# Batch 0's q and k as cast loads on the GpSimd queue, with one planner for the order: a change to a fused attention and channel-mix kernel

## The chip, the cores and the metric

The kernel runs on one core of one Trainium2 chip. The metric is the device time of one execution in microseconds (us). Shown are the median of three runs and one profiled execution, whose trace is what all times of instructions below come from.

A core has five instruction streams that matter here. TensorE (PE in the profile; its weight loads are PEld) multiplies matrices into PSUM. VectorE (DVE), ScalarE (ACT) and GpSimd (POOL) compute on tiles. SyncE (SP) only issues DMAs. POOL issues DMAs too, and it is the stream on which a DMA is issued that changes the type on its way (float32 in memory, bf16 in the tile). Each stream executes its instructions in the order in which they stand in the program.

## The reference, cut to what matters

```python
B, N, C = 4, 6208, 256
qn = q / (norm(q, axis=1) + 1e-6)          # norm over the 6208 rows, per column
kn = k / (norm(k, axis=1) + 1e-6)
a  = softmax(kn.T @ qn / tau)              # 256 x 256 for each batch
x  = v @ a                                 # 6208 x 256 for each batch
x_prev = shift x by one row (zero first)
xk = mu_k * x + (1 - mu_k) * x_prev        # xr with mu_r
out = sigmoid(xr @ w_r) * (relu(xk @ w_k) ** 2 @ w_v)
```

Each of q, k, v and the output is 4 x 6208 x 256 float32. The softmax of a batch needs all of that batch's q and k, and every row of that batch's output needs that softmax.

## The kernel before, in words

**Tiling.** Rows are handled in blocks of 512: 12 blocks per batch and 64 rows left over in each, the leftovers of the four batches together making one more block. That gives 49 blocks (`NBLK`). For a block `n`, `v_load` brings v by a cast DMA on POOL, `v_turn_pe` (first blocks) or `v_turn_dma` (later ones, a transposing DMA on SP) turns it, `x_stage` computes x = v a, `mix_stage` builds xk and xr on DVE, `up_stage` does the product with w_k, the relu on ACT and the square on DVE, `down_stage` the products with w_r and w_v, the tanh, the product and the store.

**The head.** Nothing of a block's chain can start before batch 0's softmax `A[0]`. So the kernel begins with a loop over `order0`, a list of loads of q and k of batch 0 in groups of 512 rows (28 loads; a group is 512 KB, the last k group comes in three pieces and the 64 leftover rows are small loads). Each is a float32 DMA on SP into one of ten buffers `f32s` (L280), a cast to bf16 on DVE (L291), a square on ACT or DVE (L297, L300), and products on PE: the covariance k.T q into `s_ps` (L313) and the sums of squares by a product with ones into `vr` (L306, L319), eight small products per load.

After the last q comes `inverse` and `spread` ("rq"): a power on POOL (L239, the square root of the summed squares), a few tiny steps on DVE, six small products on PE that spread q's factors over all partitions, and a copy to `rq`. After the last k, `softmax(0)`: the norms of k through POOL's L239 again, the scaling on DVE (L372), the exponential on ACT (L386), and `A[0]` on DVE (L393). Then x of block 0 (L427, copied out at L434 and L437), the mix (L467, L475, L484), and the first up product (L513).

**The other batches.** `cov_group(b, g)` loads q and k of batch `b`, group `g`, as cast DMAs on POOL (L622) into pairs made of the same buffers `f32s`, squares them on ACT (L634), adds the squares up on DVE and does products for covariance and norms (L650, L657). These are spread over the time of the earlier batch's blocks.

**What sets the order.** The program's order on every engine is written by a planner. Each step is given an engine, a duration, a key and the tiles that it reads and writes. `Plan.order` is a greedy list scheduler: whenever an engine is free in its model, it takes, of all steps whose inputs are ready, the one with the lowest key. A key is a priority, not an earliest time: a step with a late key is taken at once where the engine has nothing else that is ready. A DMA costs its engine an issue time, and its data arrive later by a bandwidth model; how many DMAs can be under way at a time is not part of the model. The steps are then put into the program in the order of their modelled starts.

In the head a fourth argument keeps steps back: the loads of v, of the weights and of batch 1 carry `after=gate_w`, which makes each of them depend on the fourth last cast of the head:

```python
gate_w = [s for s in cast_done if s.name == "cast0"][-4:-3]
gate_qk = gate_w
v_load(0, KC - 2, after=gate_w)
...
writes=[("qk", gi, x)], size=rows * n * C * 4, name="ld qk", after=list(gate_qk) + list(head))
```

Of the kernel before, what the change touches and what calls it, by code (L numbers as in the profile page):

```python
# [17 lines left out]
class Step:  # L18
    __slots__ = ("eng", "dur", "out", "key", "fn", "deps", "users", "left", "ready", "start", "seq", "size", "name")


class Plan:
# [3 lines left out]
    WAIT = {"PE": 0.3, "ACT": 0.12, "DVE": 0.12, "POOL": 0.15, "SP": 0.0}  # L26

    def __init__(self):
        self.steps = []
        self.writer = {}  # L30
        self.readers = {}

    def add(self, eng, dur, key, fn, reads=(), writes=(), size=0, name="", after=()):
        s = Step()
        s.eng, s.dur, s.key, s.fn, s.size, s.name = eng, dur, key, fn, size, name
        s.seq = len(self.steps)
        s.deps, s.users = set(after), []
        for r in reads:
            if r in self.writer:
                s.deps.add(self.writer[r])  # L40
            self.readers.setdefault(r, []).append(s)
        for w in writes:
            if w in self.writer:
                s.deps.add(self.writer[w])
            for r in self.readers.get(w, ()):
                s.deps.add(r)
            self.writer[w] = s
            self.readers[w] = []
        s.deps.discard(s)
        self.steps.append(s)  # L50
        return s

    RATE = 395e3
    MOVE = 1.3
    LAND = 0.8

    def order(self):
# [6 lines left out]
        free = {e: 0.0 for e in self.WAIT}  # L64
        waiting = {e: [] for e in self.WAIT}
        able = {e: [] for e in self.WAIT}
        bus = 0.0
# [4 lines left out]
        while len(done) < len(self.steps):  # L72
            best = None
            for e in free:
# [6 lines left out]
                if best is None or t < best[0]:  # L81
                    best = (t, e)
            t, e = best
            while waiting[e] and waiting[e][0][0] <= t:
# [4 lines left out]
            end = t + s.dur  # L89
            free[e] = end  # L90
            if s.size:
                bus = max(bus, end + self.MOVE) + s.size / self.RATE
                end = bus + self.LAND
            s.out = end
            done.append(s)
            for u in s.users:
                lag = 0.0 if s.size else (0.02 if u.eng == e else self.WAIT[e])
                u.ready = max(u.ready, end + lag)
# [7 lines left out]
def pe(n):  # L106
    return n / 2400 + 0.0025


def act(n, ptr=0):  # L110
    return 0.17 + n / 1200 + 0.09 * ptr


def dve(n, mode=1):
    return 0.16 + n / 960 / mode
# [3 lines left out]
def kernel(  # L119
# [13 lines left out]
    nc = tc.nc  # L133
# [12 lines left out]

    sb = ctx.enter_context(tc.tile_pool(name="sb", bufs=1))
# [10 lines left out]
    ones = sbuf("ones", [P])  # L158
# [9 lines left out]
    NF, NQ0, NK0 = 10, 8, 3  # L168
    f32s = ring("f32s", NF, [S, C], F32)
    q0 = ring("q0", NQ0, [S, C])  # L170
    k0 = ring("k0", NK0, [S, C])
    s0 = ring("s0", 3, [S, C])
# [13 lines left out]
    NV, NT = 4, 4  # L186
# [22 lines left out]
    T = 9.7  # L209
    KC = -2.0 * T - 8.0  # L210

    make_identity(nc, ident)
    nc.vector.memset(ones, 1.0)
    nc.vector.memset(half, 0.5)
    nc.vector.tensor_copy(ident_f, ident)

# [6 lines left out]
    LEAD = 7  # L223
# [10 lines left out]
    H0 = -100.0  # L234

    def inverse(i, key, srcn, sres, lo, hi, name):

        nres = ("nq" if lo == 0 else "nk", i)
        add("POOL", 0.8, key + .01, lambda: nc.gpsimd.tensor_tensor(nrm[i][:, lo:hi], srcn[:, lo:hi], half[:, lo:hi], op=OP.pow),  # L239
            reads=[(sres, i)], writes=[nres], name=name + " pow")  # L240
        add("DVE", dve(4), key + .02, lambda: nc.vector.tensor_scalar_add(nrm[i][:, lo:hi], nrm[i][:, lo:hi], 1e-6),
            reads=[nres], writes=[nres], name=name)
        rw = [("rrq", i)] if hi == 2 else [("rrk", i)] if lo == 2 else [("rrq", i), ("rrk", i)]
        add("DVE", dve(4), key + .03, lambda: nc.vector.reciprocal(rr[i][:, lo:hi], nrm[i][:, lo:hi]),
            reads=[nres], writes=rw, name=name)
        if inv_tau != 1.0 and hi == 4:
            add("DVE", dve(4), key + .03, lambda: nc.vector.tensor_scalar_mul(rr[i][:, 2:4], rr[i][:, 2:4], inv_tau),
                reads=[("rrk", i)], writes=[("rrk", i)], name=name)

    def spread(i, key, name):  # L250

        h, m, l = (rb[x][i] for x in range(3))
        w = [("rb", i)]
        add("DVE", dve(2), key + .04, lambda: nc.vector.tensor_copy(h, rr[i][:, 0:2]), reads=[("rrq", i)], writes=w, name=name)
        add("DVE", dve(2), key + .05, lambda: nc.vector.tensor_tensor(rd[i], rr[i][:, 0:2], h, op=OP.subtract),
            reads=[("rrq", i)] + w, writes=[("rd", i)], name=name)
        add("DVE", dve(2), key + .06, lambda: nc.vector.tensor_copy(m, rd[i]), reads=[("rd", i)], writes=w, name=name)
        add("DVE", dve(2), key + .07, lambda: nc.vector.tensor_tensor(l, rd[i], m, op=OP.subtract),
            reads=[("rd", i)] + w, writes=w, name=name)

        def go():
            for hh in range(2):
                for x, term in enumerate((h, m, l)):
                    nc.tensor.matmul(xp[:, hh * P:(hh + 1) * P], term[:, hh:hh + 1].to_broadcast([P, P]), ident,
                                     start=x == 0, stop=x == 2)
        add("PE", 6 * pe(P), key + .08, go, reads=w, writes=[("xp",)], name=name)
        add("DVE", dve(C), key + .09, lambda: nc.vector.tensor_copy(rq[i], xp[:, :C]), reads=[("xp",)], writes=[("rq", i)], name=name)

    fslot = 0
    slot0 = {}  # L270
    nsq = 0
    for i, (tn, g, j0, j1) in enumerate(order0):
        key = H0 + i
        t = q if tn == "q" else k
        rows = P if g < NB else L
        fs = fslot % NF
        fslot += 1
        f = f32s[fs]
        n = j1 - j0
        add("SP", 0.45, key, lambda f=f, t=t, g=g, j0=j0, j1=j1, rows=rows: nc.sync.dma_start(  # L280
            f[:rows, j0:j1], src(t, 0, g)[:, j0:j1, :]), writes=[("f", fs)], size=rows * n * C * 4, name="ld0")
        if tn == "q":
            ci = g % NQ0
            cast, cres = q0[ci], ("q0", ci)
        else:
            ci = g % NK0
            cast, cres = k0[ci], ("k0", ci, j0)
        wr = [cres]
        if tn == "k" and j0 == 0:
            wr = [("k0", ci, 0), ("k0", ci, 2), ("k0", ci, 3)] if g != NB - 1 else [("k0", ci, 0)]  # L290
        add("DVE", dve(n * C, 2), key, lambda f=f, cast=cast, j0=j0, j1=j1, rows=rows: nc.vector.tensor_copy(  # L291
            cast[:rows, j0:j1], f[:rows, j0:j1]), reads=[("f", fs)], writes=wr, name="cast0")
        si = nsq % 3
        nsq += 1
        s2 = s0[si]
        if tn == "k" and g < NB - 1 and g % 2 == 1:
            add("DVE", dve(n * C, 2), key + 0.5, lambda s2=s2, cast=cast, j0=j0, j1=j1, rows=rows: nc.vector.tensor_tensor(  # L297
                s2[:rows, j0:j1], cast[:rows, j0:j1], cast[:rows, j0:j1], op=OP.mult), reads=[cres], writes=[("s0", si)], name="sq0")
        else:
            add("ACT", act(n * C), key, lambda s2=s2, f=f, j0=j0, j1=j1, rows=rows: nc.scalar.activation(  # L300
                s2[:rows, j0:j1], f[:rows, j0:j1], AF.Square), reads=[("f", fs)], writes=[("s0", si)], name="sq0")
        if tn == "q":
            for j in range(j0, j1):
                def go(s2=s2, j=j, rows=rows, st=(i == 0 and j == 0)):
                    for ih in range(2):
                        nc.tensor.matmul(vr[1][:, ih:ih + 1], s2[:rows, j, ih * P:(ih + 1) * P], ones[:rows, 0:1],  # L306
                                         start=st and ih == 0, stop=False, skip_group_check=True)
                add("PE", 0.13, key + 0.3, go, reads=[("s0", si)], writes=[("vr", 1)], name="nq0")
        else:
            for j in range(j0, j1):  # L310
                def go(ci=ci, g=g, j=j, rows=rows):
                    for ih in range(2):
                        nc.tensor.matmul(s_ps[:, ih, :], k0[ci][:rows, j, ih * P:(ih + 1) * P], q0[g % NQ0][:rows, j],  # L313
                                         start=g == 0 and j == 0 and ih == 0, stop=False, skip_group_check=True)
                add("PE", 2 * pe(C), key + 0.1, go, reads=[cres, ("q0", g % NQ0)], writes=[("s_ps",)], name="cov0")

                def go(s2=s2, j=j, rows=rows, st=(g == 0 and j == 0)):
                    for ih in range(2):
                        nc.tensor.matmul(vr[0][:, ih:ih + 1], s2[:rows, j, ih * P:(ih + 1) * P], ones[:rows, 0:1],  # L319
                                         start=st and ih == 0, stop=False, skip_group_check=True)  # L320
# [452 lines left out]
```

## Time and profile before

| what | value |
|---|---|
| median of 3 runs (lowest to highest) | 528.32 us (528.12 to 529.24) |
| span of the profiled execution, first to last instruction | 526.0 us |
| what lies outside that span: median less span | 2.3 us |
| PE busy in the span | 491.1 us (93%) |
| DVE, ACT, POOL busy | 417.8 (79%), 398.5 (76%), 88.7 (17%) |
| DMA queue of POOL (q0), of SP (q1): time of their packets | 43.1%, 36.5% of 16 engines' span |
| PE busy from 60 to 510 us, from 0 to 30, from 30 to 60 | 441.3 of 450, 14.9 of 30, 23.7 of 30 |
| first up product (L513) begins | 51.22 us |

The page of a profile gives busy times, the chain of waits that ended last, and the costliest groups of instructions; the trace behind it answers for any stretch of time what every engine did and what it waited for. POOL's row counts its DMA issues (`DMA_DIRECT2D`) as work. "us to landing" is the time from the issue of a DMA to the moment at which its data are reported to be there.

### The profile page before, as it was taken

Reading aid. Unit: us, or ns where it says so; the run is one execution under the profiler, and the core shown is the slowest. Engines: PE = TensorE matmul, PEld = TensorE weight load, DVE = VectorE, ACT = ScalarE, POOL = GpSimd, SP = SyncE. Lnnn points to the kernel's source line nnn. Section 1 sums busy time; section 2 is a strip of 40 time slices with the busy share of each in tenths; the row PEclk is TensorE's granted clock in tenths of the full one; section 3 lists DMA queues with packets and bytes.
Section 4 is the critical chain, followed back from the end, with each engine's and each line's share of the span. In section 5 each row is a group of like instructions: output and inputs, shape, how many; then the busy total and the mean of one; then the engine's idle time right before and its main releaser. Section 6 shows DMA issues by size and latency. Waiting matters only on the chain.

```text
span 526.0 us, 9943 instructions
## 1 busy us (share of the span) xinstructions
PE 491.1 (93%) x3707; PEld 342.7 (65%) x3761; DVE 417.8 (79%) x970; ACT 398.5 (76%) x573; POOL 88.7 (17%) x148
## 2 busy tenths in 40 slices
PE   1785999999899999999999999999999999999996
PEld 1563777756567767666667776666666666666674
DVE  4565997788879877798888778798888887878873
ACT  6543999788789978877898868877776787777763
POOL 0054433331123233211111210010010100000000
PEclk9998999999999999999999999999999999999999
DMA  8999999999999999998758854556465563413123
GB/s 333 402 312 206 205 187 203 197 203 206 212 191 133 205 188 161 210 215 128 127 106 145 147 90 92 126 102 145 97 99 143 105 143 81 121 40 102 41 81 100
DMA packets 113944, 83.23 MB, mean 158 GB/s; under 512 B 49572, under 2 KB 101352, under 8 KB 113896
## 3 DMA queue, kind: packets, MB, share of 16 engines
q0 software_dynamic: 38160, 33.01, 43.1%
q1 hardware_dynamic: 75736, 49.59, 36.5%
q8 instruction: 29, 0.48, 0.4%
q14 instruction: 19, 0.16, 0.1%
HBM read 78.71 MB, written 25.43 MB: 198 GB/s over the span
## 4 chain that ended last, share of the span: by engine, by line
PE 77%; DVE 7%; DMA 7%; issue 4%; ACT 3%; POOL 2%; SPq 0%; ACTq 0%; POOLq 0%
PE vr L551 28%; PE kT L513 28%; PE vr L546 7%; PE xp L427 6%; PE s_ps L650 6%; DMA f32s<-in_q_dram 3%; ACT kr L516 2%; DMA f32s<-in_k_dram 2%; DMA vT<-v_bf 2%; DVE kk L518 2%; DVE dm L475 1%; DVE res L557 1%; DVE dl L467 1%; DVE xk L484 1%; POOL v_bf L335 1%
## 5 line engine op out<-in xcount | busy, mean ns | idle before, releaser
L551 PE MATMUL vr<-w_v,kk 128*128 128x256 bf16 x1552 | 251.3, 273 | 1.0
L516 ACT ACTIVATE kr<-kT 128x1024 bf16<-128x1024 f32 (+1 forms) x200 | 198.6, 1001 | 53.2 <-PE kT L513 48.3
L513 PE MATMUL kT<-xk,w_k 128*128 128x512 bf16 (+1 forms) x746 | 213.4, 372 | 7.5 <-DVE xk L484 4.5
L551 PEld LDWEIGHTS <-kk 128*128 128x128 bf16 x1552 | 149.2, 98 | 83.8 <-issue 0.4
L518 DVE TENSOR_TENSOR kk<-kr 128x1024 bf16<-128x1024 bf16 (+1 forms) x200 | 134.7, 674 | 49.2 <-ACT kr L516 47.2
L555 ACT ACTIVATE res<-vr 128x256 f32<-128x256 f32 x194 | 74.1, 387 | 37.6 <-PE vr L551 35.1
L513 PEld LDWEIGHTS <-w_k 128*128 128x128 bf16 x800 | 77.6, 98 | 33.3 <-issue 5.0
L557 DVE SCALAR_TENSOR_TENSOR res<-res,vr 128x256 f32<-128x256 f32 x194 | 80.4, 417 | 18.2 <-ACT res L555 17.2
L546 PE MATMUL vr<-w_r,xr 128*128 128x256 bf16 x388 | 72.7, 272 | 2.5 <-DVE res L557 2.2
L634 ACT ACTIVATE sq<-f32s 128x2048 bf16<-128x2048 bf16 (+1 forms) x39 | 70.8, 1816 | 0.0
L335 POOL DMA_DIRECT2D v_bf<-in_v_dram x48 | 36.8, 766 | 197.4 <-DMA vT<-v_bf 170.3
L475 DVE TENSOR_SCALAR dm<-dl,mu 128x512 bf16<-128x512 bf16 (+1 forms) x200 | 62.4, 349 | 0.6
L437 ACT CAST xR<-xp 128x512 bf16<-128x512 f32 x94 | 55.3, 589 | 7.7 <-PE xp L427 7.2
L427 PE MATMUL xp<-vT,A 128*128 128x512 bf16 x188 | 56.9, 385 | 0.1
L546 PEld LDWEIGHTS <-xr 128*128 128x128 bf16 x388 | 37.7, 98 | 19.7 <-issue 3.8
L650 PE MATMUL s_ps<-f32s 128*128 128x256 bf16 (+1 forms) x294 | 48.8, 272 | 0.1
L467 DVE TENSOR_TENSOR dl<-xR 128x1024 bf16<-128x1024 bf16 (+1 forms) x49 | 33.1, 677 | 9.2 <-ACT xR L437 9.2
L300 ACT ACTIVATE s<-f32s 128x1024 bf16<-128x1024 f32 (+3 forms) x23 | 21.1, 926 | 18.3 <-DMA f32s<-in_q_dram 9.1
L622 POOL DMA_DIRECT2D f32s<-in_q_dram x39 | 21.1, 541 | 74.0 <-ACT res L555 15.1
L484 DVE TENSOR_TENSOR xk<-dm,xR 128x1024 bf16<-128x1024 bf16 (+1 forms) x49 | 33.2, 678 | 0.3
L484 DVE TENSOR_TENSOR xr<-dm,xR 128x1024 bf16<-128x1024 bf16 (+1 forms) x49 | 33.2, 677 | 0.3
L650 PEld LDWEIGHTS <-f32s 128*128 128x128 bf16 (+1 forms) x294 | 28.0, 97 | 4.7 <-issue 0.6
(68 smaller groups left out, 237.5 us busy)
## 6 DMA issues: line engine op xcount, KB each, us to landing
out_dram<-res SPq DMA_DIRECT2D x47, 512.0 KB, 3.7
v_bf<-in_v_dram POOLq DMA_DIRECT2D x48, 256.0 KB, 6.6
f32s<-in_q_dram POOLq DMA_DIRECT2D x36, 256.0 KB, 9.6
f32s<-in_k_dram POOLq DMA_DIRECT2D x36, 256.0 KB, 9.8
f32s<-in_q_dram SPq DMA_DIRECT2D x12, 512.0 KB, 7.7
f32s<-in_k_dram SPq DMA_DIRECT2D x11, 512.0 KB, 9.5
vT<-v_bf SPq DMA_TRANSPOSE x43, 3.9
w_k<-in_moe_w_k_dram POOLq DMA_DIRECT2D x1, 512.0 KB, 8.6
```

The costliest lines, as they stand in the source:

```text
L427: nc.tensor.matmul(dst, A[b][:, ih, dh * P:(dh + 1) * P], vT[o].rearrange("p (s h) q -> p h s q", h=2)[:, ih, c0 // P:c1 // P, :], start=i ...
L475: unit(km, lambda col=col, dh=dh, c0=c0, c1=c1, km=km, w=w: add("DVE", dve(w, 4), km, lambda: nc.vector.tensor_scalar_mul(dm[di][:, dh, c0 ...
L484: nc.vector.tensor_tensor(o[which][:, :, c0:c1], dm[di][:, :, c0:c1], xR[:, :, at + c0:at + c1], op=OP.add)
L513: nc.tensor.matmul(kT[bk][:, x, :w], w_k[:, dh, fh * P:(fh + 1) * P], xk[n % 2][:, dh, c0:c1], start=dh == 0, stop=dh == 1)
L516: add("ACT", act(2 * w), ku + .1, lambda: nc.scalar.activation(kr[kri][:, :, :w], kT[bk][:, :, :w], AF.Relu, scale=0.5 ** 0.5), reads=[("k ...
L518: add("DVE", dve(2 * w, 2), ku + .2, lambda: nc.vector.tensor_tensor(kk[n % 2][:, 2 * p:2 * p + 2, c0:c1], kr[kri][:, :, :w], kr[kri][:, : ...
L546: nc.tensor.matmul(V[:, D:], xr[ri][:, dh, s * P:(s + 1) * P], w_r[:, dh, :], start=dh == 0, stop=dh == 1)
L551: nc.tensor.matmul(V[:, :D], kk[n % 2][:, fh, s * P:(s + 1) * P], w_v[:, fh, :], start=fh == 0, stop=fh == 7)
L555: add("ACT", act(D), kd + .3, lambda: nc.scalar.activation(r[:, s], V[:, D:], AF.Tanh, scale=0.5), reads=[("vr", bk)], writes=[("res", oi, ...
L557: add("DVE", 0.15 + D / 960, kd + .4, lambda: nc.vector.scalar_tensor_tensor(r[:, s], r[:, s], 1.0, V[:, :D], op0=OP.add, op1=OP.mult), re ...
L634: add("ACT", act(w), key, lambda: nc.scalar.activation(Q[:rows, :, :n], G[:rows, :, :n], AF.Square), reads=both, writes=[("sq", si)], name ...
L650: nc.tensor.matmul(s_ps[:, ih, :], G[:rows, 1, s, ih * P:(ih + 1) * P], G[:rows, 0, s, :], start=g == 0 and s == 0 and ih == 0, stop=g == ...
```

## The change

1. **Head loads.** 26 of the 28 loads of batch 0 are now cast DMAs on POOL that write bf16 into a ring `qk` of 13 pair buffers, one for each group of a batch; the first two stay float32 loads on SP with a cast on DVE. The casts of the others are gone. The same 13 pairs serve the later batches, whose `cov_group` goes on from pair 13 modulo 13. `LEAD`, by how many groups q runs ahead of k, goes from 7 to 4.
2. **Squares.** Squares of batch 0 are all on ACT, but for two pieces of the last k group on DVE. The four rows of a load are added up on DVE (two additions) before the product with ones, so that a load needs two small products in place of eight.
3. **Gates.** `gate_w` and `gate_qk` are gone: the loads of v, of the weights and of batch 1 depend only on their buffers. v has 8 buffers in place of 4, and its loads get keys 1.4 block times earlier.
4. **Fillers.** Where the model finds PE idle by more than 0.3 us between its times 20 and 48, a product of a tile of ones with itself is put in, of up to 512 columns, into `kT[0]`, which nothing reads.
5. **Block 0.** The two halves of block 0's x go to four places (`kT[1]` and `vr`) in place of two, and v of the first two blocks is turned in `xp`.
6. **The model.** A step has an occupancy and a latency, other costs and waits between engines; SP and POOL have a bus each. The block time `T` goes from 9.7 to 9.6. `make_identity` moves behind POOL's fourth head load.

```diff
-    WAIT = {"PE": 0.3, "ACT": 0.12, "DVE": 0.12, "POOL": 0.15, "SP": 0.0}
+    HOP = {"PE": 0.06, "ACT": 0.04, "DVE": 0.04, "POOL": 0.1, "SP": 0.05}
+    RATE = 400e3
+    MOVE = 1.1
+    LAND = 1.1
...
             s.start = t
-            end = t + s.dur
-            free[e] = end
+            free[e] = t + s.occ
+            end = t + s.lat
             if s.size:
-                bus = max(bus, end + self.MOVE) + s.size / self.RATE
-                end = bus + self.LAND
+                at, took = max(bus[e], end + self.MOVE), s.size / self.RATE
+                if e == "SP" and bus["POOL"] > at:
+                    bus["POOL"] += took
+                    took *= 2
+                bus[e] = at + took
+                end = bus[e] + self.LAND
...
-    NF, NQ0, NK0 = 10, 8, 3
+    NG = 13
+    NF = 2
...
-    NV, NT = 4, 4
+    NV, NT = 8, 4
...
-    LEAD = 7
+    LEAD = 4
...
+        if i < NF:
+            f = f32s[i]
+            add("SP", 0.45, key, lambda f=f, t=t, g=g: nc.sync.dma_start(f, src(t, 0, g)), ...)
+            add("DVE", dve(n * C, 2), key, lambda f=f, G=G, x=x: nc.vector.tensor_copy(G[:, x], f), ...)
         else:
+            add("POOL", 0.6, key, lambda ...: nc.gpsimd.dma_start(
+                G[:rows, x, j0:j1], src(t, 0, g)[:, j0:j1, :]), writes=[buf], size=rows * n * C * 4, name="ld0")
...
+        if n == S:
+            add("DVE", dve(2 * C, 2), key + .1, ... nc.vector.tensor_tensor(a1, s2[:, 0:2], s2[:, 2:4], op=OP.add), ...)
+            add("DVE", dve(C, 2), key + .2, ... nc.vector.tensor_tensor(a2, a1[:, 0], a1[:, 1], op=OP.add), ...)
...
+        if i == last_q:
             kq = key + 0.6
...
+            inverse(0, kq, nrm[0], "nq", 0, 2, "rq")
+            spread(0, kq, "rq")
...
+                add("POOL", 0.55, kl, lambda x=x, t=t: nc.gpsimd.dma_start(G[:rows, x, :n], src(t, b, g)),
+                    writes=[("qk", gi, x, j) for j in range(S)], size=rows * n * C * 4, name="ld qk")
...
-    gate_w = [s for s in cast_done if s.name == "cast0"][-4:-3]
-    gate_qk = gate_w
-    v_load(0, KC - 2, after=gate_w)
+    v_load(0, KC - 2)
...
+    plan.fill_from, plan.fill_to = 20.0, 48.0
+
+    def fill(n):
+        nc.tensor.matmul(kT[0][:, 0, :n], ones[:, 0:P], ones[:, :n], start=True, stop=True)
+    plan.fill, plan.fill_stop = fill, ("up", "turn v2")
...
-                kv = base - 4.6 * T
-                unit(kv, lambda n=n, kv=kv: v_load(n, kv, after=gate_w if n < NV else ()))
+                kv = base - 6.0 * T
+                unit(kv, lambda n=n, kv=kv: v_load(n, kv))
```

The keys that matter for the order on POOL: the head's loads have -200 to -173, v and weights -169 to -168.5, q's power about -178, k's power -167, the loads of batch 1's group `g` 7.2 g - 38.4, and v of block `n` 9.6 n - 57.6.

## The prediction

> **What bounds the kernel now.** The first view is the page, then busy time by stretches.
>
> ```profile
> span 526.0 us, 9943 instructions
> PE 491.1 (93%) x3707; PEld 342.7 (65%) x3761; DVE 417.8 (79%) x970; ACT 398.5 (76%) x573; POOL 88.7 (17%) x148
> ```
>
> ```profile
> 30.00:36.30 6.30, 5.81 (x44) 4.06 (x43) 4.47 (x14) 2.00 (x2) 6.22 (x9) 1.00 1.14 338
> 36.30:46.50 10.20, 6.62 (x100) 5.74 (x99) 5.88 (x17) 3.62 (x8) 3.87 (x7) 1.00 1.32 202
> 46.50:49.90 3.40, 3.18 (x11) 1.17 (x9) 0.99 (x3) 1.46 (x4) 1.82 (x3) 0.50 1.12 210
> ```
>
> The columns of the second are the stretch, the busy time of PE, PEld, DVE, ACT and POOL, the granted clock, the share and rate of the DMAs. From 60 to 510 us PE is busy 441.3 of 450 us: what comes after the first up product at 51.22 is work of PE, some 475 us of it. A change that removes none of that work can win only the 51 us ahead of it and the few us of stalls in it, and it loses what it adds to the 51. So I read the head by its chain of waits:
>
> ```profile
> 36.80 5.91 issue
> ...
> 42.75 0.72 POOL nrm L239
> ...
> 43.90 0.61 ACT e_sb L386 x2
> ...
> 46.30 0.67 PE kT L427 x3
> ...
> 50.65 0.43 DVE xk L484
> ```
>
> The power on POOL for k's norms ends at 43.47, and from there a fixed chain of 7.75 us leads to the up product. The loads are not what is late: the trace has the last data packet of batch 0's q and k at 34.96 us. PE's covariance and norm products ran on until 41.2: up to 36.25 a row of k's products and its two norm products recurred every 0.48 us, after it every 0.27.
>
> The view that decides is POOL's timeline, in which L239 and the DMA issues stand in one row:
>
> ```profile
> 30.08 0.72 POOL L239 TENSOR_TENSOR nrm<-nrm,half 128x2 f32<-128x2 f32 x1 [28.71 <-DVE nrm L324]
> 30.77 0.91 POOL L335 DMA_DIRECT2D v_bf<-in_v_dram  x1
> ...
> 34.82 0.83 POOL L335 DMA_DIRECT2D v_bf<-in_v_dram  x1
> ...
> 36.26 0.54 POOL L622 DMA_DIRECT2D f32s<-in_k_dram  x1
> 42.75 0.71 POOL L239 TENSOR_TENSOR nrm<-nrm,half 128x2 f32<-128x2 f32 x1 [5.95 <-DVE nrm L365]
> 43.43 0.57 POOL L622 DMA_DIRECT2D f32s<-in_q_dram  x1
> ...
> 45.56 0.56 POOL L622 DMA_DIRECT2D f32s<-in_q_dram  x1
> 46.55 0.54 POOL L622 DMA_DIRECT2D f32s<-in_k_dram  x1 [0.42 <-DMA v_bf<-in_v_dram]
> 47.81 0.76 POOL L335 DMA_DIRECT2D v_bf<-in_v_dram  x1 [0.72 <-DMA f32s<-in_k_dram]
> ```
>
> Brackets hold POOL's idle time and what ended it. Count the DMAs from 30.77: eight lie ahead of the second power, the 14th is the one at 46.55. It waits for a load of v although its own buffer has long been free: that load is the 6th, issued at 34.82, and the trace's landings have it at 46.27. The 15th (47.81) follows the landing of the 7th (47.53), the 17th (50.31) that of the 9th (50.02). POOL therefore has eight DMAs under way, and issue m stands still until number m-8 has landed, plus 0.3 to 0.5 us. In the backlog that sets the pace: landings 7 to 24 run from 47.53 to 69.07, 1.27 us each. Before, exactly eight issues lay between the two powers, so neither power ever waited behind a blocked issue; `gate_w` had kept the rest back.
>
> **The change part by part.** The planner's numbers are used for the order alone, times come from the trace.
>
> *How many issues stand ahead of the powers.* The model has no limit of eight; POOL issues whatever buffer is free, 0.55 to 0.9 us each. So it writes: 26 head loads (26 x 0.6, with 0.6 for the identity: to 16.2), then v, w_k, v, w_r, w_v, v (to 20.8), the clearing of a column (21.0). The keys of batch 1's loads are later, but nothing holds them: the pairs of groups 0 to 6 are free in the model by about 26, and v's buffers 3 to 7 were never used. By key it takes groups 0, 1, v3, group 2, v4, group 3, v5, groups 4, 5, v6, group 6, v7: 14 loads at 0.55 and 5 at 0.75, to 32.45. The last q lands in the model at 30.5, its square, product and copy make the power ready at 32.25. It is taken at 32.45, behind 32 + 19 = 51 DMAs. k's power is ready at 35.5 and taken at 36.0, behind groups 7, 8 and one load of 9: 56 DMAs.
>
> *When those issue on the chip.* The head is 24.25 loads of 512 KB. The first landed at 4.64 before; 23.25 more at 1.27 give 34.2, and I take 34.8, since POOL's first packets came 3.2 us after their issue at 30.77, beside which the two SP loads keep the queue busy. By packets (173 ns for 4 KB cast, 163 for 4 KB plain) it could be 36.1. Then v0 (1.35, as the next v load) and the five weights and v loads (37.77 to 46.27, 8.50): 44.65. The 43rd DMA (v5) is 11 loads later, 44.65 + 11 x 1.27 = 58.6. The 51st is issued 0.45 after it and takes 0.75: 59.8. So q's power runs to 60.5 (0.72), where it ended at 30.8 before. The 48th lands at 58.6 + 5 x 1.27 = 64.95, the 56th issues 0.45 behind it and takes 0.55: k's power runs from 66.0 to 66.7.
>
> *Who waits behind it.* Behind q's power the tiny DVE steps stop, and with them DVE's row; PE stops at the six products of `spread`, with k's last group behind them; ACT soon has no free square buffer. PE stands from some 34 to 61 us. After 60.5 there remain about 1.3 us on DVE and PE, k's eight covariance products (1.7 us at the 0.215 us of a 256-column product at half speed) and the norms, about 65, so k's power finds its input ready. Sum for the head: 66.7 - 43.47 = +23.2 us.
>
> *What the rest of the edits brings there.* From k's power to the up product were 7.75 us. x of block 0 went back into banks that ACT and DVE were still copying out: the second halves began at 47.88, after the copy of 47.40 to 47.83, 0.9 us after the first copy began, and block 1's x and its 0.59 us copy lay between. Four places end that. I take -1.5 (0 to -2.5). Casts gone (0.69 us each on DVE), six fewer small products per load, two additions more (0.42 us for 512 columns as L467's first, and no more than that for 256): all beside loads that come every 1.27 us, so nothing, and nothing if that cover went, since POOL is the one awaited. ACT's 1.06 us per square fits under 1.27 too.
>
> *Fillers.* The granted clock was 0.50 from 46.5 to 49.9, after PE stood idle for 2.15 and 0.95 us just before. A filler is at most 0.43 us at half speed. Queued behind `spread` they run in a lump after 61 us, so they neither warm PE in time nor cost over 1 us; zero, -1 to +1. The Trainium skill (TensorE: Matmul & The Clock Gate, Part 1) says that an idle window of about 3.4 us halves the clock and a busy one restores it. By that rule PE restarts cold at 61 and the last products take double, which the sum has already, and fillers that came in time would have saved about 1.7 us of the 3.4 at half clock.
>
> *After the head.* PE's work is the same. Start to start, its gaps over the columns' own time after 51.2 us come to about 12 us, some 6 of them from 105 to 160, where transposes landed 10 us late (137.70 to 148.01) in a DMA queue still full of batch 1's and 2's loads. Starting 22 us later with the same loads under way relieves that queue; the new order may do better or worse elsewhere. -2, from -5 to +4.
>
> *One rule against the change.* Loads that land every 1.27 us from POOL's queue and every 1.27 (17.58, 18.86, 20.14, 21.41) from SP's show no difference in rate. The Trainium skill (DMA: Bandwidth & Descriptors, Issuing engine by pattern) gives plain loads to SyncE as the generally faster path, and puts POOL's first byte 0.4 us later; by it the head would lose that 0.4 us once.
>
> Sum: 526.0 + 23.2 - 1.5 - 2.0 = 545.7 span, and 2.3 outside it: **548 us**.
>
> **The rivals.**
>
> *The powers do not wait (faster).* If the loads of batch 1 end up behind the powers, or POOL can pass a power by a blocked issue, the head ends with its loads: 34.8 + 1.4 (square, product, copy, power) = 36.2, so -7.3, -1.5 and -2: 526.0 - 10.8 + 2.3 = 517.5; w_v, landing at 43.3, may give some back, say 519. For it: the loads end by 35, PE has its 7 us of lag to lose. Against it: in the chain POOL waited in order in every row shown. It decides by the count: a load ahead costs 1.27 us, so 56 - 19.7/1.27 = 40 issues ahead of k's power are the point of no change, and the plan has 56.
>
> *A second hold-up later (slower still).* v loads that wait for a transpose (170.3 us in 24 waits, up to 16.6) can now stand ahead of L239 of batches 1 to 3 as well. Before, these three waited for DVE only (14.4 us). With 8 v buffers a wait that ends 5 us after the norms at each costs up to 3 x 5 = 15, less the hidden part: about 556.
>
> *The stall is shorter* by three loads counted too many or an earlier head: 541 to 544, the low end of my own range.
>
> **How the numbers follow.** Forecast 0.79, its own range 540 to 556 (count +-3 loads, 3.8 us; head -0.6 to +1.3; chain -1 to +1.5; afterwards -3 to +6). Faster rival 0.11, slower still 0.08; 0.02 near no change; all but the faster rival and that end slower, 0.87. The range 536 to 562 holds nearly all of the first and most of the third. A measurement tells about 0.2% (1 us) from no change: faster 0.11, same 0.02, slower 0.87.
>
> **What would show it.** POOL's row: 26 head issues, then v, weights and a dozen and more L622-type issues ahead of the first power, which starts near 60 instead of 30; the second near 66. PE idle from about 34 to 61, half clock at its restart, first up product near 73. After that PE as full as before. I am wrong if the first power starts before 40, if issues do not trail landings by eight, or if the first up product is before 51.

## The result, and the profile after

The changed kernel takes 561.21 us (median of 4 runs, 560.20 to 562.35), the kernel before beside it on the same chip 528.22 (527.71 to 529.24). The ratio is 1.063, with the interval 1.0609 to 1.0651: slower by 33 us. The profiled execution took 562.35 us, its span is 560.6. Ratios leave out disturbed executions, medians do not, so that for the first experiment (e1_gate) the ratio rests on runs of 537.35 and 538.58 us, while its median and its trace (548.73 us) do not.

From the page of the changed kernel, and then its busy time by stretches (stretch, busy time of PE, PEld, DVE, ACT, POOL, granted clock, share and rate of the DMAs):

```profile
span 560.6 us, 9822 instructions
PE 503.6 (90%) x3666; PEld 338.4 (60%) x3666; DVE 423.9 (76%) x987; ACT 404.3 (72%) x576; POOL 102.4 (18%) x174
```

```profile
30.00:60.00 30.00, 4.36 (x35) 2.45 (x33) 1.83 (x6) 4.08 (x6) 16.12 (x27) 0.65 1.25 201
60.00:74.50 14.50, 10.44 (x71) 6.41 (x72) 7.54 (x30) 1.74 (x6) 7.64 (x14) 0.79 1.18 207
```

PE's total didn't fall (the trace of before lacks 54 of its 800 up products, that of the change none). From 30 to 60 us PE, DVE and ACT all but stand, while the DMAs run at full share: the core is waiting for loads that nobody needs yet. POOL's timeline around the two powers shows why (in brackets POOL's idle time and what ended it):

```profile
57.81 0.53 POOL L647 DMA_DIRECT2D qk<-in_k_dram  x1 [0.71 <-DMA qk<-in_k_dram]
58.91 0.75 POOL L364 DMA_DIRECT2D v_bf<-in_v_dram  x1 [0.57 <-DMA v_bf<-in_v_dram]
59.68 0.73 POOL L247 TENSOR_TENSOR nrm<-nrm,half 128x2 f32<-128x2 f32 x1
...
66.77 0.53 POOL L647 DMA_DIRECT2D qk<-in_k_dram  x1 [0.73 <-DMA qk<-in_q_dram]
68.01 0.53 POOL L647 DMA_DIRECT2D qk<-in_q_dram  x1 [0.71 <-DMA qk<-in_k_dram]
68.55 0.72 POOL L247 TENSOR_TENSOR nrm<-nrm,half 128x2 f32<-128x2 f32 x1
```

L247 is the old L239. Neither power has an idle time of its own in brackets: each starts when the issue ahead of it ends, and that issue waited for a landing. 51 DMAs stand ahead of the first power, 58 ahead of the second. The waits of the changed kernel (who waited for whom: us in total, times, longest) say the same from the other side:

```profile
DVE nrm L249 <- POOL nrm L247: 31.1, 5, 26.7
PE xp L272 <- DVE rb L262: 26.4, 1, 26.4
POOL nrm L247 <- DVE acc L689: 11.9, 3, 11.0
```

One wait of 26.7 us is q's power of batch 0. The last line is L247 of batches 1 to 3: it waited for its input, as before, so there was no second hold-up. The chain of waits ahead of the first up product:

```profile
57.81 9.66 DMA qk<-in_k_dram
...
68.01 0.53 POOL qk L647
68.55 0.73 POOL nrm L247
...
74.03 0.43 DVE xk L515
```

Loads of batch 1, whose softmax comes over 100 us later, are the path. The first up product begins at 74.51, before at 51.22.

The second part of the loss is less visible: from the first up product to the end of the span it takes 486.1 us, before 474.8. I measured PE's gaps there: the distance from the start of one product to the start of the next, less the columns' own time (products missing from a trace taken out at 0.216 us each). Table 1 has them for all kernels; "early" is the first 120 us after the first up product. Which products are missing has to be inferred, so the early gaps are uncertain by about 1 us, e5's by up to 3. Medians are of all runs of a kernel.

| kernel | powers start at | first up product | span after it | gaps early, later | median us |
|---|---|---|---|---|---|
| before | 30.1, 42.8 | 51.2 | 474.8 | 6.4, 6.3 | 528.2 |
| after (the change) | 59.7, 68.6 | 74.5 | 486.1 | 9.1, 13.4 | 561.2 |
| e1_gate | 35.7, 40.5 | 47.1 | left out | left out | 543.7 |
| e2_actsqrt | 34.6, 38.7 (ACT) | 45.0 | 496.4 | 17.0, 15.1 | 545.9 |
| e3_dose | 44.9, 50.6 | 56.6 | 496.6 | 17.1, 14.8 | 555.0 (1 run) |
| e4_before_nogate | 31.1, 48.7 | 63.5 | 483.0 | 16.6, 6.4 | 548.3 (1 run) |
| e5_oldmodel | 35.5, 39.3 | 48.1 | 496.4 | 24.0, 7.0 | 544.9 |
| e7_depth | 35.5, 41.0 | 47.1 | 484.8 | 8.4, 12.8 | 534.7 |
| e8_depth_old | 35.5, 39.2 | 48.3 | 483.0 | 13.5, 6.3 | 530.2 |
| e9_nofill | 36.3, 40.8 | 46.9 | 493.5 | 14.6, 15.2 | 537.5 |
| e10_after_oldcosts | 60.9, 72.4 | 80.0 | 482.4 | 13.2, 6.3 | 565.3 |
| e11_before_places | 29.9, 43.1 | 49.9 | 476.0 | 7.8, 6.3 | 527.3 |
| e12_early | 33.2, 38.5 | 45.5 | 487.5 | 16.9, 6.4 | 533.8 |
| e13_reach8 | 35.5, 39.2 | 46.6 | 471.5 | 5.5, 3.2 | 520.8 |

For the change, gaps grew by 2.7 early and by 7.1 later; about 0.9 us is x work that now lies after the first up product.

### The profile page after: what moved, and what is told of

It is laid out like the page before. It is cut to its first block, busy times and chain, and to the rows that moved or that the text cites. A ratio compares the mean times of both kernels' runs of the same rounds, so it can differ in the third digit from the quotient of the medians.

```text
span 560.6 us, 9822 instructions
## 1 busy us (share of the span) xinstructions
PE 503.6 (90%) x3666; PEld 338.4 (60%) x3666; DVE 423.9 (76%) x987; ACT 404.3 (72%) x576; POOL 102.4 (18%) x174
## 4 chain that ended last, share of the span: by engine, by line
PE 62%; DVE 14%; DMA 13%; issue 4%; ACT 4%; POOL 2%; POOLq 0%; ACTq 0%
PE kT L544 23%; PE vr L582 23%; DMA qk<-in_k_dram 10%; PE vr L577 6%; PE xp L457 5%; PE s_ps L675 4%; DVE dm L506 3%; DVE kk L549 3%; DVE xk L515 2%; DVE dl L499 2%; ACT kr L547 2%; DMA vT<-v_bf 1%; DVE res L588 1%; DMA v_bf<-in_v_dram 1%; DVE xr L515 1%
## 5 line engine op out<-in xcount | busy, mean ns | idle before, releaser
L547 ACT ACTIVATE kr<-kT 128x1024 bf16<-128x1024 f32 (+1 forms) x200 | 197.2, 1001 | 55.9 <-PE kT L544 50.6
L582 PE MATMUL vr<-w_v,kk 128*128 128x256 bf16 x1552 | 215.0, 273 | 1.5 <-DVE kk L549 1.1
L544 PE MATMUL kT<-xk,w_k 128*128 128x512 bf16 (+1 forms) x800 | 201.8, 375 | 4.3 <-DVE xk L515 2.9
L582 PEld LDWEIGHTS <-kk 128*128 128x128 bf16 x1552 | 149.9, 98 | 38.5 <-DVE kk L549 7.2
L588 DVE SCALAR_TENSOR_TENSOR res<-res,vr 128x256 f32<-128x256 f32 x194 | 78.6, 415 | 11.1 <-ACT res L586 10.9
L577 PE MATMUL vr<-w_r,xr 128*128 128x256 bf16 x388 | 74.0, 272 | 1.2 <-DVE res L588 1.2
L659 ACT ACTIVATE sq<-qk 128x2048 bf16<-128x2048 bf16 (+1 forms) x39 | 71.0, 1821 | 0.0
L675 PE MATMUL s_ps<-qk 128*128 128x256 bf16 (+1 forms) x294 | 42.9, 272 | 1.1 <-DVE e_sb L401 1.1
L499 DVE TENSOR_TENSOR dl<-xR 128x1024 bf16<-128x1024 bf16 (+1 forms) x49 | 33.2, 678 | 10.8 <-ACT xR L467 10.6
L647 POOL DMA_DIRECT2D qk<-in_q_dram x39 | 20.9, 537 | 66.8 <-ACT res L586 20.2
L675 PEld LDWEIGHTS <-qk 128*128 128x128 bf16 (+1 forms) x294 | 27.3, 97 | 7.0 <-issue 2.2
L279 ACT ACTIVATE sq<-qk 128x1024 bf16<-128x1024 bf16 (+2 forms) x26 | 24.0, 976 | 8.8 <-DMA qk<-in_q_dram 5.6
```

Of the source, the lines that this page charges most:

```text
L544: nc.tensor.matmul(kT[bk][:, x, :w], w_k[:, dh, fh * P:(fh + 1) * P], xk[n % 2][:, dh, c0:c1], start=dh == 0, stop=dh == 1)
L547: add("ACT", act(2 * w), ku + .1, lambda: nc.scalar.activation(kr[kri][:, :, :w], kT[bk][:, :, :w], AF.Relu, scale=0.5 ** 0.5), reads=[("k ...
L577: nc.tensor.matmul(V[:, D:], xr[ri][:, dh, s * P:(s + 1) * P], w_r[:, dh, :], start=dh == 0, stop=dh == 1)
L582: nc.tensor.matmul(V[:, :D], kk[n % 2][:, fh, s * P:(s + 1) * P], w_v[:, fh, :], start=fh == 0, stop=fh == 7)
L588: add("DVE", dve(D), kd + .4, lambda: nc.vector.scalar_tensor_tensor(r[:, s], r[:, s], 1.0, V[:, :D], op0=OP.add, op1=OP.mult), reads=[("v ...
L659: add("ACT", act(w), key, lambda: nc.scalar.activation(Q[:rows, :, :n], G[:rows, :, :n], AF.Square), reads=both, writes=sqs, name="sq")
```

## The experiments

### The head: is it the place of the powers?

The theory: a power waits for the DMA issues ahead of it, eight under way, 1.27 us a load. The rival: the cast loads or the squares of the new head are themselves late.

**e1_gate.** In the changed kernel, batch 1's loads and the later first loads of v depend on k's power; 32 DMAs are left ahead of each power.

```diff
+    gate_k = [s for s in plan.steps if s.name == "chain pow"][:1]
-  ... name="ld qk")
+  ... name="ld qk", after=gate_k if b == 1 else ())
-  v_load(n, kv)
+  v_load(n, kv, after=gate_k if n < NV else ())
```

> The changed kernel with one thing put back: batch 1's loads and the v loads from block 3 on depend on the power for k's norms of batch 0, so 32 DMAs stand ahead of both powers in place of 51 and 58. Theory (a power waits in POOL's row behind issues of which each waits for the landing of the one eight before): the 32nd issue follows the landing of the 24th at about 34.1 us, so the first power runs at 35 to 36 us, the second at 38 to 40 us, the first up product begins at 44 to 46 us (74.5 in the changed kernel), and the time falls by about 29 us to 530 to 534 us. If the later loads, started some us later, cost nothing. Rival (the loss lies in the new order of the whole program and the powers only show it): the time stays above 550 us. Second rival (all of the 33 us is the powers): 519 us or less.

**e3_dose.** The same gate, but groups 0 to 2 of batch 1 and one load of v are let through: 39 ahead of both.

> As the kernel with 32 DMAs ahead of the powers, but the first three groups of batch 1 and one more block of v are let through: 39 DMAs ahead of both powers. Theory: the 39th issue follows the landing of the 31st (w_v), which landed at 43.2 us in the changed kernel, so the first power runs at 44.3 to 45.5, the second 2 to 4 us later, the first up product begins at 53 to 55 us and the time is 8 to 10 us above that kernel's, near 541. Rival (a power waits for any DMA to be under way at all, or only for the bandwidth): no more than 3 us above that kernel.

**e2_actsqrt.** The changed kernel, POOL's row of DMAs as it is; only batch 0's two powers become square roots on ACT.

```diff
-  add("POOL", (0.8, 0.9), ..., nc.gpsimd.tensor_tensor(nrm, srcn, half, op=OP.pow))
+  add("ACT", (0.3, 0.4), ..., nc.scalar.activation(nrm, srcn, AF.Sqrt))
```

> The changed kernel with the two powers of batch 0 on ACT as a square root in place of POOL; POOL's row of DMAs stays as it is, word for word, without the two powers. Theory (the place in POOL's row): the root of q's norms runs near 33 us, that of k's near 36 to 38, the first up product begins at 42 to 46 us in spite of the same loads being under way, and the time falls to 527 to 533 us; function tables to load on ACT cost some 1.3 us each time, as at 0.74 us before. Rival (the loads of batch 1 that are under way, their share of the DMA engines, or PE's cold restart hold the head up): the first up product stays beyond 60 us and the time above 548.

Measured: ratios to before 1.0176 (1.015 to 1.0202) for e1 and 1.0304 (1.0249 to 1.0358) for e2; e3 took 554.96 us in one run. POOL's timeline of e1_gate, then of e3_dose, then ACT's of e2_actsqrt:

```profile
35.63 0.16 POOL L441 MEMSET xR<- 128x2 bf16 x1
35.69 0.77 POOL L247 TENSOR_TENSOR nrm<-nrm,half 128x2 f32<-128x2 f32 x1
40.50 0.70 POOL L247 TENSOR_TENSOR nrm<-nrm,half 128x2 f32<-128x2 f32 x1 [4.04 <-DVE nrm L394]
```

```profile
44.37 0.53 POOL L647 DMA_DIRECT2D qk<-in_k_dram  x1 [2.11 <-DMA w_v<-in_moe_w_v_dram]
44.92 0.74 POOL L247 TENSOR_TENSOR nrm<-nrm,half 128x2 f32<-128x2 f32 x1
```

```profile
34.58 0.20 ACT L248 ACTIVATE nrm<-nrm 128x2 f32<-128x2 f32 x1
38.72 0.20 ACT L248 ACTIVATE nrm<-nrm 128x2 f32<-128x2 f32 x1 [2.68 <-DVE nrm L398]
```

With 32, 39 and 51 issues ahead, q's power starts at 35.7, 44.9 and 59.7. From 39 to 51 that is 1.23 us an issue, the landing rate. Off POOL, with all 51 issues in their place, its input is there before 34.6. So the new head's loads and squares are not late, and the stall of some 25 us is the place of the powers. This part is shown by position, by dose and by removal.

But the totals fell short. e2 has its first up product 29.5 us earlier than the change, and ends only 19.2 us earlier by span (541.4 to 560.6): the rest of the kernel takes 10.3 us longer, 496.4 in place of 486.1. The stall had hidden something.

**e4_before_nogate.** The kernel before, with batch 1's loads let go of their gate (`gate_qk = []`), nothing else.

> The kernel before with one edit: the loads of batch 1 no longer depend on the head's fourth last cast. 2 DMAs stand ahead of the first power and 17 ahead of the second (0 and 8 before), and v0 and w_k come 11th and 12th. Theory (eight under way): the 17th issue follows the landing of the 9th, near 45 us, so the second power runs at 45.5 to 48 us (42.75 before), w_k lands near 50, the first up product begins at 53 to 56 us and the time is 2 to 5 us above the kernel before. Rival (a load ahead of a power costs nothing by itself): 527 to 530 us.

Measured: 548.27 us, +20 where a few were expected. 2 and 17 DMAs now stand ahead of the powers. The chain of waits of e4:

```profile
48.72 0.73 POOL nrm L239
...
50.97 5.41 ACT sq L634 x3
...
56.40 0.69 DVE t L637
```

k's power is 6 us later, and then three squares of batch 1 (L634, 1.8 us each) stand on ACT ahead of block 0's copies, and DVE's sum of them ahead of the turn of v: from the power's end to the up product 14.0 us, before 7.75. With the gaps (16.6 early) that makes the 20. My expectation priced only the issues. In this one run the gate was worth some 20 us to the old kernel: it kept back not only issues, but the work that follows the loads.

### After the head: the planner's costs, or the reach of the loads?

**e5_oldmodel.** e1 with the planner's costs, waits, bandwidth model and T of before.

```diff
-    HOP = {"PE": 0.06, "ACT": 0.04, "DVE": 0.04, "POOL": 0.1, "SP": 0.05}
+    HOP = {"PE": 0.3, "ACT": 0.12, "DVE": 0.12, "POOL": 0.15, "SP": 0.0}
-    T = 9.6
+    T = 9.7
... (pe, act, dve and the buses likewise)
```

> As the kernel with 32 DMAs ahead of the powers, but with the planner's durations, waits between engines, bandwidth model and block time of before (9.7 for T), so that only the order of the program differs from it. After its first up product the changed kernel has 22.5 us of gaps on PE where the kernel before has 12.3, most of them around the softmax of batches 1 to 3. Theory (the finer model's order brings them): 4 to 10 us below the kernel with 32 ahead, gaps on PE after the first up product of 12 to 17 us. Rival (the deeper loads and the 8 buffers of v bring them, or the late start of batch 1's loads): within 2 us of that kernel.

**e7_depth.** e1, new costs, but the reach of before: 4 buffers of v with keys `base - 4.6 * T`, and a pair load held until the covariance of the group ten before it.

```diff
-    NV, NT = 8, 4
+    NV, NT = 4, 4
+            hold = used.get(nl[0] - 10, ())
```

> As the kernel with 32 DMAs ahead of the powers, with the loads' reach of before put back: 4 buffers of v and their keys of before, and a load of q, k waits for the covariance of the group ten before (ten pairs in use at a time instead of 13). The model stays the new one. That kernel began its first up product at 47.1 us and then had 32 to 35 us of gaps on PE, 16 to 17 of them in the first 120 us, in which SP's transposes and stores landed 10 to 20 us after their issue beside a POOL queue that never ran dry. Theory (the loads that reach further ahead take the DMA engines from transposes and stores): first up product still at 45 to 48 us, gaps in the 120 us after it 6 to 11 us, time 527 to 533. Rival (an early start of the blocks alone starves them, at any reach): gaps as before the edit and a time of 536 to 540.

**e8_depth_old.** Both.

> As the kernel with the reach of before, with the planner's costs and block time of before as well: of the change there remain the cast loads of the head, the squares summed ahead, the fillers and block 0's places. Theory (the finer model's order costs some 8 us around the softmax of batches 1 to 3, where the gaps from 120 us after the first up product on are 14 to 15 us with the new costs and 6 to 7 with the old): 5 to 9 us below the kernel with the reach of before alone, 520 to 527 us, which is faster than the kernel before. Rival (the order's share depends on where the loads land, not on the model): within 2 us of that kernel.

**e10_after_oldcosts.** The change itself, no gate, with the costs and T of before.

> The changed kernel with the planner's costs, waits, bandwidth model and block time of the kernel before; no gate. 52 and 61 DMAs stand ahead of the two powers (51 and 58 in the changed kernel), so by eight under way and 1.27 us a load the powers should start near 61 and 72.4, and the first up product near 78 (+3.8). Theory that the new costs made the order around the softmaxes of batches 1 to 3 worse: PE's gaps later than 120 us after the first up product fall from 13 to 15 us to 7 or 8, which takes 6 to 8 us: 557 to 559 us. Rival, that these gaps come from the further reach of the loads (13 pairs, 8 buffers of v): no fall, 565 us.

Measured: e5 544.86 us, ratio 1.0303 (1.0275 to 1.0331); e7 534.70, 1.012 (1.0078 to 1.0163); e8 530.17, 1.0044 (1.0023 to 1.0066); e10 565.30, 1.0698 (1.0677 to 1.0718). e7 ended just above what was expected; e5, e8 and e10 missed theirs by more. In the totals it is the reach that counts: the reach of before takes the ratio from 1.0303 to 1.0044 with the old costs (e5, e8) and from 1.0176 to 1.012, with intervals that overlap, with the new ones (e1, e7). The old costs gain only where the reach is short (e7 to e8, 4.5 us); they lose in e1 (1.0176 to 1.0303, e5) and in the change (1.063 to 1.0698, e10).

Yet Table 1's last but one column shows what the costs do. With the reach of before or that of the change, later gaps are 6.3 to 7.0 us in every kernel with the old costs (before, e4, e5, e8, e10, e11, e12), and 12.8 to 15.2 in every one with the new costs (after, e2, e3, e7, e9). So the new costs lose about 6 to 8 us beyond the first 120 us, whatever the head does; e10 took just this out of the change: 13.4 to 6.3. Reach has a part in these gaps too: e13 below, with the old costs and a shorter reach, has 3.2. PE's timeline at batch 1's softmax shows one such place, though there it still lies within the first 120 us; first the change, then e10:

```profile
185.13 0.50 PE L272 MATMUL xp<-ident,rb 128*128 128x128 bf16 x6
185.58 0.39 PE L582 MATMUL vr<-w_v,kk 128*128 128x256 bf16 x2
186.90 0.24 PE L682 MATMUL xp<-ones,t 128*128 128x1 bf16 x4 [0.93 <-DVE rq L275]
187.69 1.03 PE L675 MATMUL s_ps<-qk 128*128 128x256 bf16 x8 [0.55 <-DVE e_sb L401]
```

```profile
195.74 0.50 PE L268 MATMUL xp<-ident,rb 128*128 128x128 bf16 x6
196.07 0.60 PE L540 MATMUL kT<-xk,w_k 128*128 128x512 bf16 x2
196.50 0.38 PE L573 MATMUL vr<-w_r,xr 128*128 128x256 bf16 x2
196.72 1.04 PE L578 MATMUL vr<-w_v,kk 128*128 128x256 bf16 x8
197.59 0.24 PE L678 MATMUL xp<-ones,t 128*128 128x1 bf16 x4
```

`spread` writes `xp`, DVE must copy it out to `rq`, and the next norm product writes `xp` again. In the change the plan leaves two products of cover between them, and PE stands 0.93 us, then 0.55 for `s_ps`; in e10, 12 products lie between and nothing waits. In the later stretch the change has the same two waits at batch 2's softmax:

```profile
311.92 0.24 PE L682 MATMUL xp<-ones,t 128*128 128x1 bf16 x4 [0.67 <-DVE rq L275]
312.71 1.03 PE L675 MATMUL s_ps<-qk 128*128 128x256 bf16 x8 [0.55 <-DVE e_sb L401]
```

These two are some 1.5 of the 7.1 us, start to start. Within 12 us of the softmaxes of batches 2 and 3 the change has 5.6 us of gaps and e10 has 1.9; the rest of the difference is spread over the blocks. Nor do these two waits come with the new costs alone: e8, with the old ones, has them at batch 1's softmax (0.30 and 0.69 us, at 165.7 and 166.6). Which of the costs takes the cover away was not tested.

Early gaps went the other way (e5 24.0, e10 13.2), which is why the totals missed. e10 also lost in the head: 52 and 61 issues ahead gave 60.9 and 72.4, as worked out, but the first up product came at 80.0, not 78.

**e13_reach8.** e8, with a pair load held until the covariance of the group eight before.

```diff
-            hold = used.get(nl[0] - 10, ())
+            hold = used.get(nl[0] - 8, ())
```

> The same version (530.2 us), with a pair load of q and k held until the covariance of the group eight before, in place of ten: the loads reach two groups less far ahead. Powers and first up product unchanged (35.5, 39.2, 48.3). Theory that loads which reach far ahead delay the transposes: PE's gaps between 30 and 90 us after the first up product, 9.6 us, fall to 4 or 5: 525 to 527 us. Rival, that reach has no part in it: 530 us.

Measured: 520.81 us (519.88 to 520.92), ratio 0.9855 (0.9839 to 0.987). It beats both kernels, by 8 us the one before. The two traces differ by more than the medians, since e8's is an execution of 533.07 us and e13's one of 519.88. Between them the early gaps fell from 13.5 to 5.5 (my expectation had put e8's at 9.6, from 30 to 90 us on), the later ones from 6.3 to 3.2, and the first up product came 1.7 us earlier. The theory is only part of it. Chains of waits of e8_depth_old and of e13_reach8 around 100 us:

```profile
93.70 9.96 DMA qk<-in_q_dram
103.66 22.13 DMA vT<-v_bf
125.83 1.01 PE xp L453 x2
```

```profile
96.71 20.44 DMA vT<-v_bf
117.20 0.62 PE xp L453 x2
```

The same transpose takes 22.1 and 20.4 us: this one is hardly faster with the shorter reach. It starts 7 us earlier, because its load of v was issued at 86.5 in place of 89.3 and landed at 96.7 in place of 103.6. The DMA issues from 60 to 130 us (count, KB each, median us to landing), e8 and then e13:

```profile
qk<-in_q_dram POOLq DMA_DIRECT2D x14, 256.0 KB, 12.2
qk<-in_k_dram POOLq DMA_DIRECT2D x14, 256.0 KB, 12.7
...
v_bf<-in_v_dram POOLq DMA_DIRECT2D x7, 256.0 KB, 14.2
vT<-v_bf SPq DMA_TRANSPOSE x6, 16.3
```

```profile
qk<-in_q_dram POOLq DMA_DIRECT2D x12, 256.0 KB, 12.4
qk<-in_k_dram POOLq DMA_DIRECT2D x12, 256.0 KB, 12.4
v_bf<-in_v_dram POOLq DMA_DIRECT2D x9, 256.0 KB, 11.0
vT<-v_bf SPq DMA_TRANSPOSE x8, 12.8
```

Four loads for the next batch gave way to two loads of v for the blocks at hand. In the median v landed in 11.0 us in place of 14.2, and the transposes in 12.8 in place of 16.3, as the theory has it. Earlier issue and shorter time to landing thus came together, and the runs don't part them. It is the head's fault once more: one queue in program order, and what is needed soon stands behind what is needed late.

### Single edits

**e11_before_places.** The kernel before; the second halves of block 0's x go to `vr`.

```diff
-  dst = xp[:, c0:c1] if n else kT[0][:, dh, c0:c1]
+  dst = xp[:, c0:c1] if n else vr[dh][:, :256] if ci else kT[0][:, dh, c0:c1]
```

> The kernel before with one edit of the change: the second halves of block 0's x go to vr in place of kT[0], so they need not wait until the first halves are copied out. Powers stay at 30.1 and 42.8. If the wait for the copies is worth what the chain says, the stretch from k's power to the first up product falls from 7.75 to 6 us or so: 526 to 527 us. Rival: the chain is given back in a later stall, 528 us.

Measured: 527.34 us, ratio 0.9977 (0.9967 to 0.9986). From the end of k's power (43.8) to the up product (49.9) it takes 6.1 us, as expected; by the medians 1.45 us of the 1.66 were kept, by the interval 0.7 to 1.7.

**e12_early.** e8, with v's first loads and the weights behind q's power: 26 and 32 ahead.

> The version with the powers ahead of batch 1's loads, the reach of before and the costs of before (530.2 us), and besides the first loads of v and the weights behind q's power: 26 and 32 DMAs ahead of the powers in place of 32 and 32. q's power should start at 30.5 to 32 in place of 35.5, k's at 36.5 to 38 in place of 39.2, the first up product at 46 to 47.5 in place of 48.3. If it is kept: 528 to 529.5 us. Rival: an earlier first block meets the same late transposes, so that PE's gaps grow by what the head wins: 530 to 532.

Measured: 533.76 us, ratio 1.0093 (1.0072 to 1.0114), 3.6 us slower than e8. The first up product came 2.8 us earlier (45.5), the rest took 4.5 us longer, with early gaps of 16.9 in place of 13.5: the rival. A head that is ready sooner meets the same late transposes: PE's longest gap there, 4.5 us at 119, ends with a transpose.

**e9_nofill.** e7 without fillers (`plan.fill_to` 0).

> As the kernel with the reach of before, without fillers. Theory (fillers are worth the half clock that they avoid in the head, no more): the granted clock is half for longer between 36 us and the first up product, which begins 0.5 to 2 us later; the time is 0 to 2 us above that kernel's. Rival (fillers hold up real work on PE): 0 to 2 us below it.

Measured: 537.54 us (534.38 to 542.05), ratio 1.0182 (1.0123 to 1.024); e7's runs reach from 532.14 to 536.99. The first up product is at 46.9 without fillers and at 47.1 with them: half clock fell into 25.0 to 35.2 without and into 38.0 to 41.4 with them, and the head was no longer for it. What differs lies in the gaps afterwards, and that fillers cause it, the runs don't show.

## Why the prediction was right, and which term was not

The sign, the mechanism and its place were right; the time lies at the high end of the range and outside the forecast's own 540 to 556. Term by term, in us (the 2.3 outside the span were 1.75):

| term | forecast | measured |
|---|---|---|
| DMAs ahead of the powers | 51, 56 | 51, 58 |
| last head load landed; the 43rd DMA landed | 34.8; 58.6 | 34.77; 58.63 |
| q's power starts | 59.8 | 59.68 |
| k's power ends, against 43.47 before | 66.7 (+23.2) | 69.27 (+25.8) |
| k's power to first up product, against 7.75 | -1.5 | 5.24 (-2.5) |
| span after it, against 474.8 | -2.0 | 486.1 (+11.3) |
| span | 545.7 | 560.6 |

The forecast missed the span by 14.9 us: 2.6 in the head, -1.0 in the chain, 13.3 after it.

*The count and the rule of eight.* Counting issues in the model's order and letting each wait for the landing of the eighth before it put q's power within 0.2 us. That rule came from three pairs of an issue and a landing in the kernel before; in the change each of POOL's 9th to 60th issues came at least 0.28 us after the landing eight before it. Two issues more than counted ahead of k's power, at 1.27 us, are its 2.5.

What the eight is, the trace tells too: POOL's 159 DMAs report their landings on eight semaphores in turn, SP's on eight others, and each issue waits for the one that it will use itself. So eight is what this program gives each stream; that the queue would take no more is not shown.

The point of no change, 40 issues, was put too high for the head: with 39 ahead (e3) the first up product came 5.4 us later than before, since k's power followed q's only 5.7 us later (50.6 and 44.9).

*The chain.* e11 prices the four places at 1.7 by itself, inside the 0 to 2.5. Another 0.8 or so came from the turn of block 1's v, whose 0.67 us copy had lain between the two halves of `A[0]` and was moved behind block 0's x.

*Loads at one rate from both queues.* I set the Trainium skill's rule (DMA: Bandwidth & Descriptors, Issuing engine by pattern) against the rows and took the rows. No loss by the path showed: POOL's first load landed at 7.08, 1.25 us behind SP's last one (5.83). That the last head load landed within 0.03 us of my 34.8 is in part luck. I had added 0.6 for late first packets on POOL, which cost nothing; 0.6 was lost elsewhere, at a load that landed 1.84 us behind the one before it (30.57 after 28.73).

*A reading that was wrong.* Batch 0's loads in the kernel before did not end at 34.96: the last two pieces of k landed at 36.53 and 37.31, their last packet of data at 36.92. The forecast took nothing from it, but PE's lag behind the loads, which a faster head could win, was 4 us and not 7, and the change's head loads ended 2.5 us earlier than before.

*Fillers.* PE's timeline of the change after its 26 us wait:

```profile
61.08 1.21 PE L272 MATMUL xp<-ident,rb 128*128 128x128 bf16 x6 [26.45 <-DVE rb L262]
...
65.38 3.51 PE L722 MATMUL kT<-ones 128*128 128x512 bf16 x14
```

These 14 ran in a lump, while POOL still held k's power back, and cost nothing: PE then stood 2.06 us for `A[0]`. The granted clock was 0.50 from 38.7 to 66.0: it fell 4.1 us after PE stopped at 34.6 and came back 4.9 us after it restarted. The Trainium skill (TensorE: Matmul & The Clock Gate, Part 1) has windows of about 3.4 us in both directions; the trace agrees to within one window.

*The step that failed* is "After the head": -2, from -5 to +4, measured +11.3. I had argued that 22 us more of loading relieves the queue. One part of the loss is shown to come from the new planner costs: the 7.1 us of later gaps, which are gone with the old costs (e10, 6.3), though early gaps then grow, so that e10's stretch is only 3.7 us shorter (482.4). About half of the 7.1 lies around the softmaxes of batches 2 and 3 (5.6 us of gaps against 1.9). The rest of the loss, 2.7 us of early gaps, 0.9 of x work and 0.6 elsewhere, wasn't taken apart in the changed kernel. I had seen that its order differed everywhere, and allowed it 4 us; the waits for `rq` and for `xp` at a softmax, which could have priced some of it, I left out of the sum.

*The relief was real within the new order, but hid behind the stall*: with the stall gone, e2's early gaps are 17.0 in place of 9.1 (6.4 in the kernel before). So the rival "the powers do not wait: 519 us" was wrong too. Its condition was made true in e1 and e2, and they took 537 and 542 us at best. It had priced the head and kept the rest; 519 needs the reach and the costs put back as well, and e13, with the head of the change, the old costs and a reach of eight, reached 520.8.

## What to carry to other kernels

A queue executed in program order makes each long-lead prefetch a possible blocker of what stands behind it, compute included. Count the issues ahead of each instruction that is on the path, by how many can be under way (here eight, the program's own semaphores), before a dependency that looks like mere throttling is dropped. And after a stall has been removed, measure the stretch behind it again: transfers that were early enough may no longer be so, and there a prefetch that reaches less far may pay (9.4 us here, by one 10 that became an 8).

## What the runs showed of the hardware that I had not expected

Transposes and stores on SP's queue landed slowly while POOL's queue was full of loads. Over a whole execution the 32 to 34 blocks' transposes with a landing in the trace took 6.1 us on average before, 6.2 in e8 and e13, with longest times of 20.8, 22.9 and 20.1, where the shortest take 2.7. With the change's reach and no stall they took longer: 9.2 in e1 and 8.4 in e2. In the changed kernel, with the head's 22 us of loading ahead, stores averaged 4.0 us, before 5.8. And ten microseconds of half clock, from 25 to 35 us in e9's head, cost its first up product nothing: PE waited for loads there, once for 1.72 us.
